# The least chosen score found by VectorE alone: a search in shares, with a threshold per partition, in six of eight batches

## The chip, the cores and the metric

The kernel runs on one core of a Trainium2 chip. The metric is the device time of one execution in microseconds. TensorE multiplies matrices into PSUM, VectorE, ScalarE and GpSimd work on tiles in SBUF, and SyncE issues nearly all transfers, in the order of its own queue.

## The reference

Eight batches of 3136 tokens. Each goes through an attention without softmax, and 128 of its tokens, those with the highest gate score, through a small network of two layers.

```python
scores = scale * np.matmul(z, z.transpose(0, 2, 1))     # z: 8 x 3136 x 64
attn = np.maximum(scores, 0.0) ** 2
x = u * np.matmul(attn, v)                              # u, v: 8 x 3136 x 256
gate = np.einsum('bsd,d->bs', x, w_gate)
for b in range(B):
    top_idx = np.argpartition(-gate[b], capacity)[:capacity]      # capacity 128
    xe = x[b, top_idx]
    ye = np.maximum(xe @ w1, 0.0) @ w2                  # 256 -> 1024 -> 256
    g = 1.0 / (1.0 + np.exp(-gate[b, top_idx]))
    out[b, top_idx] = x[b, top_idx] + g[:, None] * ye
```

## The kernel before

A batch is cut into seven chunks of output tokens: five of 512, one of 256 and one of 320. A chunk walks over all 3136 tokens in thirteen slots: twelve of two groups of 128 tokens and one of the last 64. In a slot TensorE multiplies the squared scores with `v` into `acc` (L523), with `hi` and `lo`, the two parts of each score, and in between computes the raw scores `sc` of the slot three ahead (L417). ScalarE takes these through a relu (L427) and rounds their square to `hi` (L428); VectorE squares them exactly (`a`, L438) or ScalarE does (L433), by what the planner thinks each has to do; VectorE or GpSimd subtracts to get `lo` (L487). Scores are symmetric, so VectorE also transposes squares that a later chunk needs (`aT`, L456, L475), they are stored (`squares`, `squares_narrow`, `squares_own`) and fetched there as old pairs, which need no score matmul. The score banks in PSUM are two, `acc` has three, and one bank, `misc`, is left for all small work.

The end of a chunk (`finish`) multiplies with `u`, transposes, stores and adds up the gate scores of its tokens; these are near tasks, in slots 2 and 5 of the next chunk. When a batch's last chunk is through, `route(b)` gives a list of far tasks, which run in the slots of the next batch: at most one per slot, none in a chunk's last slot, none in a slot with a near task, and after each a distance in slots that the list itself names (two where it names none). A task has matmuls, mixed into those of the slot, and posts, work for the other engines, put out around the work on the slot's scores (`settle_scores`): of several, the first half ahead of it and the rest behind; of one, it is ahead. Posts of the slot before a chunk's last one are held for that last one. The order on each engine is the order of issue. `spend` tells the planner what an engine was given, which decides between VectorE, ScalarE and GpSimd for squares and subtractions.

The search for the 128th highest score, in `route`: `fold` (L686) brings the scores of a batch into 98 rows of 32 and `start` copies them to `G`. Eight rounds then settle four bits each of the score's pattern. `tries` (L703) makes fifteen thresholds, `count` compares 98x15x32 elements (`ge`, L710) and adds up along each row (`cnt`, L718), `total` (L724) sums the rows with one matmul of a matrix of ones, and `settle` counts how many thresholds still have 128 scores or more (L729, L733) and appends that digit to `base` (L746 or L748). A round is one task with the distance three: `total`, then `settle` and `tries`, then `count`. After the last one come `masks` (which scores are above, which equal) and `run_up`, then `ahead`, `quotas`, `spans`, `take`, and the expert stage `expert` with its gather, two layers and scatter.

Batch 7 is different (`merged`): its last four chunks are searched late, and its first three through this search on 96 rows of 16. Batch 6 has its tasks at a distance of two, and the later part of batches 5 and 6's experts is held for the end.

Of the kernel before, what the change touches and what calls it, by code (L numbers as in the profile page):

```python
# [18 lines left out]
P = 128  # L19
# [21 lines left out]
def constants(S, cap):  # L41
# [35 lines left out]
    steps = np.arange(1, 1 << BITS, dtype=np.int64)  # L77
# [4 lines left out]
    return [np.concatenate(cols[dt], 1) for dt in (F32, BF16)], at, np.tile(keys, (rows, 1))  # L82


@with_exitstack
def attention_then_routed_ffn(ctx: ExitStack, tc: tile.TileContext, zt, ut, v, wg, w1, w2, cst, cst16, keys, outs, at, cap):
# [13 lines left out]
    NF = F // P  # L100
    SCALE = 1.0 / S
    NS = (1 << BITS) - 1
    SLOTS = NJ // 2 + 1

    const = ctx.enter_context(tc.tile_pool(name="const", bufs=1))
# [9 lines left out]
    def misc_bank(name):  # L115
        return ps_m.tile([P, 512], F32, name=name, tag="misc")
# [10 lines left out]
    def load_consts():  # L127
        c_sb = const.tile([P, cst.shape[1]], F32, name="c_sb")
        nc.sync.dma_start(c_sb, cst)
        k_sb = const.tile([TP, keys.shape[1]], I32, name="k_sb")  # L130
# [200 lines left out]
        for i in range(2)  # L331
    ]
    own = [[tc.dram_tile([P, GT, P], F32, name=f"squares_own{i}_{c}") for c in range(WHOLE)] for i in range(2)]

    def is_first(k):
        b, c, js, _ = slots[k]
# [329 lines left out]
    def route(b):  # L666
# [29 lines left out]

        def tries(rd):
            f = st["ps"][:R, 128 : 128 + NS]
            k = consts["keys"][:R, rd * NS : (rd + 1) * NS]
            if rd == 0:  # L700
                nc.vector.tensor_copy(f, k.bitcast(F32))
            else:
                nc.vector.tensor_scalar(f.bitcast(I32), k, st["base"], None, op0=ALU.bitwise_xor)  # L703
            st["f"] = f
            spend(dve=0.2)

# [15 lines left out]
        def total():  # L722
            st["ps"] = misc_bank("tot")
            nc.tensor.matmul(st["ps"][:R, :NS], ones, st["n"], start=True, stop=True)  # L724

        def settle(rd):
            junk = moe.tile([TP, NS], F32, name="enough", tag="enough")[:R]
            m = moe.tile([TP, 1], F32, name="m", tag="m")[:R]
            nc.vector.tensor_scalar(  # L729
                junk, st["ps"][:R, :NS], float(cap), None, op0=ALU.is_ge, op1=ALU.add, accum_out=m  # L730
            )
            mi = moe.tile([TP, 1], I32, name="mi", tag="mi")[:R]
            nc.vector.tensor_copy(mi, m)  # L733
            base = moe.tile([TP, 1], I32, name="base", tag="base", bufs=2)[:R]
            if rd == last:
                base = st["ps"][:R, 64:65].bitcast(I32)
            if rd == 0:
                k = moe.tile([TP, 1], I32, name="place", tag="place")[:R]
                nc.vector.tensor_scalar(
                    k, mi, 32 - BITS, INT_MIN, op0=ALU.logical_shift_left, op1=ALU.bitwise_xor  # L740
                )
                flip = moe.tile([TP, 1], I32, name="flip", tag="flip")[:R]
                nc.vector.tensor_scalar(
                    flip, k, 31, 0x7FFFFFFF, op0=ALU.arith_shift_right, op1=ALU.bitwise_and
                )
                nc.vector.tensor_tensor(base, k, flip, op=ALU.bitwise_xor)  # L746
# [5 lines left out]
            spend(dve=0.6)  # L752

        def masks():
            t = st["base"].bitcast(F32).broadcast_to([R, NT])
# [90 lines left out]
        for rd in range(last):  # L846
            tasks.append(([total], [lambda rd=rd: (settle(rd), tries(rd + 1)), count], 3))
        if late:
            tasks.append(([total], [lambda: settle(last), masks]))
            tasks += [([columns], keep_columns), ([places], ranks)]  # L850
            tasks += choose(st, 0, cap)
            choice[b] = st
        else:
            tasks.append(([total], [lambda: settle(last), masks, run_up]))
# [612 lines left out]
```

## Time and profile before

| | |
|---|---|
| time, median of 3 runs | 2091.34 us (2090.43 to 2091.94) |
| profiled execution, its own time | 2093.4 us |
| its span | 2091.6 us |
| TensorE busy | 2074.4 us, 99% |
| VectorE busy | 1511.1 us, 72% |
| GpSimd busy | 1370.5 us, 66% |
| ScalarE busy | 1278.5 us, 61% |
| mean DMA rate over the span | 196 GB/s |

Busy times are unions of an engine's instructions over one profiled execution. PE is TensorE, PEld its weight load, DVE VectorE, ACT ScalarE, POOL GpSimd, SP or SPq SyncE and its queue. L724 is line 724 of the kernel. "x4" is a count of instructions. In a timeline, a bracket gives the engine's idle time just before the instruction and what ended it. Matmuls are pipelined, so their durations overlap: distances are read from start to start.

### The profile page before, as it was taken

The page shows a single profiled execution, that of the slowest core. Times are in us where ns is not written, and L with a number is a line of the kernel's source. Part 1 is how long each engine was busy: PE and PEld are TensorE (multiplying, and loading weights), DVE is VectorE, ACT ScalarE, POOL GpSimd, SP SyncE. Part 2 cuts the span into 40 slices and gives each one's busy share as a digit, 9 for nine tenths or more (in the row PEclk, how much of TensorE's full clock was granted, in tenths as well). Part 3 has the DMA queues.
Part 4 walks back from the last instruction along what each step waited for, and adds up shares of the span by engine and source line. Part 5 has one row for each costly group of instructions (what it writes and reads, how often), then busy time and mean ns, then how long its engine had stood idle before and what let it go on. Part 6 is the DMA issues. An engine that isn't in the chain of part 4 may idle for free.

```text
span 2091.6 us, 31263 instructions
## 1 busy us (share of the span) xinstructions
PE 2074.4 (99%) x10359; PEld 1749.5 (84%) x10359; DVE 1511.1 (72%) x2334; ACT 1278.5 (61%) x1619; POOL 1370.5 (66%) x729
## 2 busy tenths in 40 slices
PE   9999999999999999999999999999999999999998
PEld 6888978889888898888988889888898888878788
DVE  8766678766777667875678757786577876787776
ACT  7665577656765467664676546765477655775543
POOL 6666677656866478764776647865578655765643
PEclk9999999999999999999999999999999999999999
DMA  6788767786668866688667876678776786666862
GB/s 190 201 242 212 206 184 214 217 229 173 188 188 222 216 184 189 185 221 217 183 192 190 228 206 188 186 199 224 199 200 180 192 194 184 186 181 168 216 168 94
DMA packets 408771, 409.66 MB, mean 196 GB/s; under 512 B 129120, under 2 KB 320416, under 8 KB 405536
## 3 DMA queue, kind: packets, MB, share of 16 engines
q1 hardware_dynamic: 407552, 405.30, 71.4%
q0 software_dynamic: 768, 2.10, 0.3%
q8 instruction: 81, 1.33, 0.3%
q14 instruction: 82, 0.67, 0.1%
q10 hardware_dynamic: 288, 0.26, 0.0%
HBM read 235.31 MB, written 172.23 MB: 195 GB/s over the span
## 4 chain that ended last, share of the span: by engine, by line
PE 81%; DMA 6%; POOL 4%; issue 3%; ACT 2%; DVE 2%; SPq 1%; POOLq 0%; ACTq 0%; DVEq 0%
PE acc L523 67%; PE sc L417 12%; DMA vst<-in_v 4%; POOL lo L487 2%; POOL V L121 1%; ACT a L427 1%; DVE a L438 1%; ACT hi L428 1%; PE h L1106 1%; PE y L1150 1%; SPq L274 1%; DMA vst<-in_w 1%; POOL ZL L121 1%; DMA squares_narrow<-aT 0%; DVE aT L456 0%
## 5 line engine op out<-in xcount | busy, mean ns | idle before, releaser
L523 PE MATMUL acc<-hi,V 128*128 128x512 f32 (+2 forms) x5376 | 1224.9, 366 | 3.2 <-DVE ut L568 1.0
L487 POOL TENSOR_TENSOR lo<-a,hi 128x1024 fp32r<-128x1024 f32 (+1 forms) x335 | 748.8, 2238 | 597.3 <-DVE a L438 443.1
L523 PEld LDWEIGHTS acc<-hi,V 128*128 128x128 f32 x5376 | 929.4, 188 | 166.3 <-DVE ut L568 5.9
L523 PE MATMUL acc<-lo,V 128*128 128x512 f32 (+2 forms) x2688 | 664.1, 363 | 0.0
L427 ACT ACTIVATE a<-sc 128x1024 f32<-128x1024 f32 (+4 forms) x408 | 363.0, 890 | 488.2 <-PE sc L417 364.8
L438 DVE TENSOR_TENSOR a<-sc,a 128x1024 f32<-128x1024 f32 (+3 forms) x334 | 338.4, 1013 | 289.8 <-ACT hi L428 261.3
L523 PEld LDWEIGHTS acc<-lo,V 128*128 128x128 f32 x2688 | 471.4, 188 | 76.7 <-POOL lo L487 1.5
L395 ACT CAST hi<-qk 128x1024 fp32r<-128x1024 f32 (+2 forms) x320 | 276.1, 863 | 234.8 <-PE acc L523 205.7
L456 DVE STREAM_TRANSPOSE aT<-a 128x512 f32<-128x512 f32 (+1 forms) x520 | 341.1, 691 | 101.0 <-ACT a L433 69.9
L428 ACT ACTIVATE hi<-a 128x1024 fp32r<-128x1024 f32 (+4 forms) x408 | 377.4, 925 | 18.7 <-PE acc L523 2.1
L487 DVE TENSOR_TENSOR lo<-qk,hi 128x1024 fp32r<-128x1024 f32 (+2 forms) x212 | 335.8, 1594 | 54.3 <-ACT hi L395 52.3
L417 PE MATMUL sc<-Z,ZH 128*128 128x512 f32 (+2 forms) x760 | 281.9, 375 | 4.8 <-DVE a L438 4.5
L417 PE MATMUL sc<-Z,ZL 128*128 128x512 f32 (+2 forms) x760 | 278.2, 370 | 0.7 <-DVE ZL L121 0.7
L487 POOL TENSOR_TENSOR lo<-qk,hi 128x1024 fp32r<-128x1024 f32 (+2 forms) x108 | 203.2, 1884 | 51.8 <-ACT hi L395 40.9
L417 PEld LDWEIGHTS sc<-Z,ZH 128*128 128x128 f32 x760 | 142.6, 188 | 39.2 <-DVE a L438 12.0
L417 PEld LDWEIGHTS sc<-Z,ZL 128*128 128x128 f32 x760 | 142.6, 188 | 25.2 <-DVE ZL L121 1.1
L121 POOL TENSOR_TENSOR V<-vst,V 128x512 fp32r<-128x512 f32 x89 | 139.7, 1579 | 13.9 <-ACT V L120 13.4
L589 POOL TENSOR_TENSOR ut<-x,w_run 128x1024 f32<-128x1024 f32 (+2 forms) x52 | 130.0, 2499 | 15.9 <-DVE x L580 14.9
L433 ACT ACTIVATE a<-a 128x1024 f32<-128x1024 f32 x74 | 78.6, 1062 | 2.4
L568 DVE SCALAR_TENSOR_TENSOR ut<-acc,ut 128x512 f32<-128x512 f32 (+2 forms) x112 | 64.0, 612 | 19.5 <-PE acc L523 19.2
L121 POOL TENSOR_TENSOR ZL<-zst,ZH 128x512 fp32r<-128x512 f32 (+2 forms) x56 | 73.5, 1317 | 2.4 <-ACT ZH L120 2.1
L120 ACT CAST V<-vst 128x512 fp32r<-128x512 f32 x95 | 57.8, 609 | 21.1 <-DMA vst<-in_v 20.8
(175 smaller groups left out, 1039.1 us busy)
## 6 DMA issues: line engine op xcount, KB each, us to landing
squares<-aT SPq DMA_DIRECT2D x160, 512.0 KB
qk<-squares SPq DMA_DIRECT2D x320, 256.0 KB
squares_narrow<-aT SPq DMA_DIRECT2D x320, 128.0 KB
qk<-squares_narrow SPq DMA_DIRECT2D x80, 512.0 KB
vst<-in_v SPq DMA_DIRECT2D x190, 128.0 KB
out<-x SPq DMA_DIRECT2D x162, 128.0 KB
ut<-in_ut SPq DMA_DIRECT2D x40, 512.0 KB
squares_own<-aT SPq DMA_DIRECT2D x39, 256.0 KB
```

The lines of the kernel that those rows point to most:

```text
L121: (lo_on or nc.vector.tensor_tensor)(lo, src, hi.bitcast(F32), op=ALU.subtract)
L395: nc.scalar.copy(by(hi), src)
L417: nc.tensor.matmul(ps[:, q], z[:, j * P : (j + 1) * P], mov, start=z is ZH, stop=z is ZL)
L427: nc.scalar.activation(a, ps[:, :n], AF.Relu)
L428: nc.scalar.activation(pieces[0][0](hi), pieces[0][1], AF.Square)
L433: nc.scalar.activation(a, a, AF.Square)
L438: square = lambda: nc.vector.tensor_tensor(a[rows], ps[rows, :n], a[rows], op=ALU.mult)
L456: nc.vector.transpose(to, a[rows, q].rearrange("p (m t a) -> p m t a", t=GT, a=Q))
L487: on.tensor_tensor(view(lo), src, view(hi).bitcast(F32), op=ALU.subtract)
L523: nc.tensor.matmul(ac[h], w, mov, start=first and h not in started, stop=stop)
L568: nc.vector.scalar_tensor_tensor(xT[:, h, :w], acc[b, c][h], SCALE * SCALE, xT[:, h, :w], op0=ALU.mult, op1=ALU.mult)
L589: nc.gpsimd.tensor_tensor(wx, runs, consts["wg_run"].rearrange("p (o r) -> p o r", o=1).broadcast_to([P, NB, RUN]), op=ALU.mult,)
```

## The change

For batches 0 to 5 the search takes another form. The scores are stored to DRAM (`set_out`) and loaded back so that each of eight shares of 392 scores lies on sixteen partitions (`bring_back`). Each of the sixteen has a threshold of its own (the last one is not counted). A round is two tasks. `count_shares` compares a share with a threshold on each of 128 partitions and accumulates the count, then brings the 128 counts into each of 32 partitions by four 32x32 transposes. `settle_shares` adds up the eight shares, compares with 128, counts, appends the digit to the base, and makes the next threshold of each partition with four xors of 32 partitions. Its sums lie in the `misc` bank, written by VectorE. No matmul is in a round. The distance is one slot behind a count and one or two behind a settle.

Batches 6 and 7 keep the old form, but `tries` shifts one row of steps instead of reading shifted ones.

```diff
-    keys = np.concatenate(keys).astype(np.uint32).view(np.int32)
+    own = np.stack(keys, 1)
+    own[-1] = 0
+    own = np.tile(own, (P >> BITS, 1))
+    keys = np.concatenate([own, np.tile(np.append(keys[0], steps), (P, 1))], 1).astype(np.uint32).view(np.int32)
...
+        def set_out():
+            nc.vector.tensor_copy(G, st["ps"][:R, :NT])
+            stores.append(lambda: nc.sync.dma_start(scores_there[b % 2].rearrange("(r t) -> r t", t=NT), G))
+
+        def bring_back():
+            n = S // SHARES
+            st["row"] = moe.tile([P, 4, P], F32, name="gates", tag="hh", bufs=2).rearrange("p f r -> p (f r)")[:, :n]
+            for g in range(SHARES):
+                src = scores_there[b % 2][g * n : (g + 1) * n].rearrange("(o t) -> o t", o=1)
+                nc.sync.dma_start(st["row"][g << BITS : (g + 1) << BITS], src.broadcast_to([1 << BITS, n]))
+            st["least"] = consts["keys"][:, 0:1].bitcast(F32)
+
+        def count_shares():
+            big = moe.tile([P, 512], F32, name="ge", tag="big", bufs=2)
+            own = moe.tile([P, 1], F32, name="own", tag="m")
+            nc.vector.tensor_scalar(
+                big.bitcast(BF16)[:, : S // SHARES], st["row"], st["least"], None,
+                op0=ALU.is_ge, op1=ALU.add, accum_out=own,
+            )
+            st["n"] = big[:Q, 512 - P :]
+            for q in range(0, P, Q):
+                nc.vector.transpose(st["n"][:, q : q + Q], own[q : q + Q].broadcast_to([Q, Q]))
+            spend(dve=1.5)
+
+        def settle_shares(rd):
+            ps = misc_bank("tot")
+            n, enough = ps[:Q, : NS + 1], ps[:Q, 32 : 32 + NS]
+            nc.vector.tensor_reduce(n, st["n"].rearrange("p (g s) -> p s g", s=NS + 1), axis=AX.X, op=ALU.add)
+            nc.vector.tensor_scalar(enough, n[:, :NS], float(cap), None, op0=ALU.is_ge)
+            mi = moe.tile([Q, 1], I32, name="mi", tag="mi")
+            with nc.allow_low_precision(reason="whole numbers"):
+                nc.vector.tensor_reduce(mi, enough, axis=AX.X, op=ALU.add)
+            shift = 32 - BITS * (rd + 1)
...
+            base = moe.tile([Q, 1], I32, name="base", tag="base", bufs=2)
+            if rd == 0:
+                first_base(base, mi, Q)
+            else:
+                nc.vector.tensor_scalar(base, mi, shift, st["base"], op0=ALU.logical_shift_left, op1=ALU.bitwise_xor)
+            least = moe.tile([P, 1], I32, name="least", tag="least", bufs=2)
+            for q in range(0, P, Q):
+                nc.vector.tensor_scalar(
+                    least[q : q + Q], consts["keys"][:Q, rd + 1 : rd + 2], base, None, op0=ALU.bitwise_xor
+                )
+            st["base"] = base
+            st["least"] = least.bitcast(F32)
+            spend(dve=1.65)
...
-        last = 32 // BITS - 1
-        tasks = [([fold], [start, count], 3)]
+        last = ROUNDS - 1
+        by_shares = not late and not (put_off(b) and b == B - 2)
+        if by_shares:
+            tasks = [([fold], set_out, 2), ([], bring_back, 2)]
+            for rd in range(last):
+                tasks += [([], count_shares, 1), ([], lambda rd=rd: settle_shares(rd), 1 + rd % 2)]
+            tasks += [([], count_shares, 1), ([], [lambda: settle_shares(last), lambda: (masks(), run_up())], 2)]
+        else:
+            tasks = [([fold], [start, count], 3)]
+            for rd in range(last):
+                tasks.append(([total], [lambda rd=rd: (settle(rd), tries(rd + 1)), count], 3))
```

`first_base` holds the three instructions that `settle` had for round 0. The last settle writes its base to four groups of 32 partitions in PSUM, for `masks`, which stays as it was.

## Rows read from the trace of the kernel before

**Rows 1.** The profile's page: busy us of each engine with its share of the span and count of instructions, and the shares of the chain that ended last by engine.

```profile
PE 2074.4 (99%) x10359; PEld 1749.5 (84%) x10359; DVE 1511.1 (72%) x2334; ACT 1278.5 (61%) x1619; POOL 1370.5 (66%) x729
...
PE 81%; DMA 6%; POOL 4%; issue 3%; ACT 2%; DVE 2%; SPq 1%; POOLq 0%; ACTq 0%; DVEq 0%
```

**Rows 2.** The waits of TensorE over the whole span: who waited for whom, us in total, times, longest.

```profile
PE sc L417 <- DVE a L438: 4.5, 9, 0.8
...
PE tot L724 <- DVE cnt L718: 1.1, 2, 0.8
```

**Rows 3.** The timeline of TensorE in batch 1's search: start, us, line, operation.

```profile
574.00 1.07 PE L523 MATMUL acc<-lo,V 128*128 128x512 f32 x4
574.91 0.17 PE L724 MATMUL tot<-cnt,c 98*98 98x15 bf16 x1
...
576.86 0.39 PE L417 MATMUL sc<-Z,ZH 128*128 128x512 f32 x1
...
577.78 1.07 PE L523 MATMUL acc<-lo,V 128*128 128x512 f32 x4
...
580.50 0.39 PE L417 MATMUL sc<-Z,ZH 128*128 128x512 f32 x1
```

**Rows 4.** The instructions of the tile `tot` on TensorE (duration in ns: least, median, most; first and last start in us), and from the timeline the last one of batch 5's search (the 48th of the 64) and the first two of batch 6's.

```profile
L724 PE MATMUL tot<-cnt,c x64: 169/173/175, 309.7 to 1990.3; 98*98 98x15 bf16 x56, 96*96 96x15 bf16 x8
...
1664.48 0.17 PE L724 MATMUL tot<-cnt,c 98*98 98x15 bf16 x1
...
1831.71 0.17 PE L724 MATMUL tot<-cnt,c 98*98 98x15 bf16 x1 [0.77 <-DVE cnt L718]
...
1839.27 0.17 PE L724 MATMUL tot<-cnt,c 98*98 98x15 bf16 x1 [0.37 <-DVE cnt L718]
```

**Rows 5.** Groups of VectorE by line and shape: the search's instructions. Busy us, mean ns of one, then the idle time before them.

```profile
L718 DVE TENSOR_REDUCE cnt<-ge 98x15 bf16<-98x480 bf16 x56 | 36.7, 656 | 1.9
...
L710 DVE TENSOR_TENSOR ge<-G,tot 98x480 bf16<-98x480 f32 x49 | 30.2, 617 | 0.0
...
L703 DVE TENSOR_SCALAR tot<-k_sb,base 98x15 int32<-98x15 int32 x49 | 11.6, 237 | 1.7
...
L748 DVE TENSOR_SCALAR base<-mi,base 98x1 int32<-98x1 int32 x42 | 9.0, 214 | 1.5
L733 DVE CAST mi<-m 98x1 int32<-98x1 f32 x56 | 8.6, 154 | 1.9
L729 DVE TENSOR_SCALAR_CACHE_REDUCE enough<-tot 98x15 f32<-98x15 f32 x56 | 8.6, 153 | 4.6 <-PE tot L724 4.3
...
L729 DVE DVE_READ_ACCUMULATOR enough<-tot 98x1 f32 x56 | 4.5, 81 | 0.0
```

**Rows 6.** The nearest shapes to the new instructions: from the same view a compare with accumulation of 384 columns and a reduction of 240, and from the views of the tiles `aT`, `mi` and `base` (duration in ns: least, median, most; first and last start) the transposes, the shift with xor of one column (L748) and the xor of two tiles (L746).

```profile
L954 DVE TENSOR_SCALAR_CACHE_REDUCE beats<-row,col 128x384 bf16<-128x384 f32 x4 | 2.4, 598 | 0.0
...
L718 DVE TENSOR_REDUCE cnt<-ge 96x15 bf16<-96x240 bf16 x8 | 3.2, 401 | 0.3
...
L456 DVE STREAM_TRANSPOSE aT<-a x520: 662/702/717, 19.1 to 2013.5; 128x512 f32<-128x512 f32 x162, 64x512 f32<-64x512 f32 x12
...
L475 DVE STREAM_TRANSPOSE aT<-a x78: 399/418/447, 58.2 to 1980.4; 128x256 f32<-128x256 f32 x78
...
L748 DVE TENSOR_SCALAR base<-mi,base x48: 210/214/216, 318.8 to 1978.8; 98x1 int32<-98x1 int32 x42, 96x1 int32<-96x1 int32 x6
...
L746 DVE TENSOR_TENSOR base<-place,flip x8: 156/681/1727, 313.8 to 1953.4; 98x1 int32<-98x1 int32 x7, 96x1 int32<-96x1 int32 x1
```

**Rows 7.** Busy time by stretch: the stretch and its length, then busy us (and count) of PE, PEld, DVE, ACT and POOL, the granted clock, the DMA share and GB/s. First a stretch of batch 0's search, a part of batch 1's, and all of batch 6's; then the sum over the seven searches of batches 0 to 6, 83 us each and 65 for the last.

```profile
314.00:391.00 77.00, 77.00 (x347) 63.01 (x347) 63.06 (x120) 51.37 (x58) 56.86 (x28) 1.00 0.71 199
585.00:605.00 20.00, 20.00 (x92) 16.40 (x92) 18.52 (x31) 11.94 (x15) 13.75 (x7) 1.00 0.79 210
1823.00:1888.00 65.00, 63.86 (x285) 51.18 (x284) 53.97 (x110) 45.30 (x52) 42.26 (x24) 1.00 0.62 176
...
sum 563.00, PE 561.86 PEld 458.20 DVE 461.24 ACT 377.16 POOL 386.50; mean PE 80.27 PEld 65.46 DVE 65.89 ACT 53.88 POOL 55.21
```

**Rows 8.** The timeline of a score bank in the second chunk of batch 1's search: the scores, the relu, the square, and the score matmul two groups on, which takes the same bank.

```profile
597.63 0.39 PE L417 MATMUL sc<-Z,ZH 128*128 128x512 f32 x1
...
598.80 1.03 ACT L427 ACTIVATE a<-sc 128x1024 f32<-128x1024 f32 x1 [2.03 <-PE sc L417]
...
601.01 1.23 DVE L438 TENSOR_TENSOR a<-sc,a 128x1024 f32<-128x1024 f32 x1 [0.16 <-ACT hi L428]
...
604.50 0.39 PE L417 MATMUL sc<-Z,ZH 128*128 128x512 f32 x1
```

**Rows 9.** The timeline of SyncE's queue, and below it of VectorE, around the end of the first chunk after batch 0.

```profile
304.41 4.08 SPq L470 DMA_DIRECT2D squares_narrow<-aT  x6
310.85 0.34 SPq L477 DMA_DIRECT2D squares_own<-aT  x1
316.00 0.52 SPq L462 DMA_DIRECT2D squares<-aT  x1
...
310.05 0.77 DVE L475 STREAM_TRANSPOSE aT<-a 128x256 f32<-128x256 f32 x2 [0.96 <-DMA squares_narrow<-aT]
...
317.12 1.29 DVE L456 STREAM_TRANSPOSE aT<-a 128x512 f32<-128x512 f32 x2
```

**Rows 10.** The timeline of SyncE's queue: four loads of 64 KB issued one after the other.

```profile
329.82 2.02 SPq L385 DMA_DIRECT2D vst<-squares_own  x4
```

More of the change, by code (lines that the diff above doesn't have):

```diff
@@ L76, in constants @@
     put("tok_late16", tok.reshape(P, -1), BF16)
-    steps = np.arange(1, 1 << BITS, dtype=np.int64)
+    steps = np.arange(1, (1 << BITS) + 1, dtype=np.int64)
     keys = [(steps << sh) & 0xFFFFFFFF for sh in range(32 - BITS, -1, -BITS)]
@@ L80, in constants @@
     keys[0] = np.where(keys[0] >> 31, keys[0] ^ 0x7FFFFFFF, keys[0])
-    keys = np.concatenate(keys).astype(np.uint32).view(np.int32)
-    return [np.concatenate(cols[dt], 1) for dt in (F32, BF16)], at, np.tile(keys, (rows, 1))
+    own = np.stack(keys, 1)
+    own[-1] = 0
+    own = np.tile(own, (P >> BITS, 1))
+    keys = np.concatenate([own, np.tile(np.append(keys[0], steps), (P, 1))], 1).astype(np.uint32).view(np.int32)
+    return [np.concatenate(cols[dt], 1) for dt in (F32, BF16)], at, keys
 @with_exitstack
@@ L102, in attention_then_routed_ffn @@
     NS = (1 << BITS) - 1
+    ROUNDS = 32 // BITS
+    SHARES = P >> BITS
     SLOTS = NJ // 2 + 1
@@ L129, in load_consts @@
         nc.sync.dma_start(c_sb, cst)
-        k_sb = const.tile([TP, keys.shape[1]], I32, name="k_sb")
+        k_sb = const.tile([P, keys.shape[1]], I32, name="k_sb")
         nc.sync.dma_start(k_sb, keys)
@@ L333, in attention_then_routed_ffn @@
     own = [[tc.dram_tile([P, GT, P], F32, name=f"squares_own{i}_{c}") for c in range(WHOLE)] for i in range(2)]
+    scores_there = [tc.dram_tile([S], F32, name=f"scores{i}_there") for i in range(2)]
     def is_first(k):
@@ L724, in total, with first_base @@
             nc.tensor.matmul(st["ps"][:R, :NS], ones, st["n"], start=True, stop=True)
+        def first_base(base, mi, n):
+            k = moe.tile([TP, 1], I32, name="place", tag="place")[:n]
+            nc.vector.tensor_scalar(k, mi, 32 - BITS, INT_MIN, op0=ALU.logical_shift_left, op1=ALU.bitwise_xor)
+            flip = moe.tile([TP, 1], I32, name="flip", tag="flip")[:n]
+            nc.vector.tensor_scalar(flip, k, 31, 0x7FFFFFFF, op0=ALU.arith_shift_right, op1=ALU.bitwise_and)
+            nc.vector.tensor_tensor(base, k, flip, op=ALU.bitwise_xor)
         def settle(rd):
@@ L737, in settle @@
             if rd == 0:
[L738 to L746, printed above, removed]
+                first_base(base, mi, R)
             else:
@@ new lines, in settle_shares @@
+        def settle_shares(rd):
[7 more added lines that the diff above has]
+            shift = 32 - BITS * (rd + 1)
+            if rd == last:
+                least = ps[:, 64:65].bitcast(I32)
+                for q in range(0, P, Q):
+                    nc.vector.tensor_scalar(
+                        least[q : q + Q], mi, shift, st["base"], op0=ALU.logical_shift_left, op1=ALU.bitwise_xor
+                    )
+                st["base"] = least[:R]
+                spend(dve=1.45)
+                return
+            base = moe.tile([Q, 1], I32, name="base", tag="base", bufs=2)
[4 more added lines that the diff above has]
+            least = moe.tile([P, 1], I32, name="least", tag="least", bufs=2)
+            for q in range(0, P, Q):
+                nc.vector.tensor_scalar(
+                    least[q : q + Q], consts["keys"][:Q, rd + 1 : rd + 2], base, None, op0=ALU.bitwise_xor
+                )
+            st["base"] = base
+            st["least"] = least.bitcast(F32)
+            spend(dve=1.65)
@@ L840, in take @@
             nc.tensor.matmul(st["ps"][:, : NT + 2], st["of"], st["taken"], start=True, stop=True)
-        last = 32 // BITS - 1
-        tasks = [([fold], [start, count], 3)]
+        last = ROUNDS - 1
[9 more added lines that the diff above has]
+                tasks.append(([total], [lambda rd=rd: (settle(rd), tries(rd + 1)), count], 3))
         if late:
             tasks.insert(0, ([], [lambda: bring_weight(1), halve]))
-        for rd in range(last):
-            tasks.append(([total], [lambda rd=rd: (settle(rd), tries(rd + 1)), count], 3))
-        if late:
             tasks.append(([total], [lambda: settle(last), masks]))
@@ L853, in route @@
         else:
-            tasks.append(([total], [lambda: settle(last), masks, run_up]))
+            if not by_shares:
+                tasks.append(([total], [lambda: settle(last), masks, run_up]))
             tasks.append(([ahead], [quotas, lambda: spans(0)], 3))
```

7 lines of the change are left out of this document (4 added, 3 removed).

## The prediction

> **What bounds the kernel now.** I read the busy times first. TensorE is busy for 2074.4 of a span of 2091.6 us, VectorE for 1511.1 (72%) [rows 1]; the chain of work that ended last is TensorE for 81% of its length [rows 1]. The reader is to see that nothing but TensorE's own stream can give a microsecond back, unless another engine makes it wait. Next I read TensorE's waits. The largest is the score matmuls waiting for VectorE's square, 4.5 us in 9 waits; the search's own matmul (`tot`) waited 1.1 us in two [rows 2], and both of those lie in the search that keeps the old form [rows 4]. So in the six batches of the change no wait on the search is to be won: the search costs TensorE only what its matmuls occupy. Third I read one such matmul in its surroundings, and last VectorE's load in the stretch where the search runs.
>
> **What is removed from TensorE.** Each round has one 98x15 matmul, 64 in the kernel; the six changed batches hold 48 of them, the first at 309.7 us and the last at 1664.48 [rows 4]. The busy row says 0.17 us for one, but it overlaps its neighbours, so I take start to start. With it, from the four `lo` matmuls at 574.00 to the next score matmul at 576.86, it is 2.86 us; the same sequence without it, one slot on, runs from 577.78 to 580.50, 2.72 us [rows 3]. The price is 0.14 us, most of it behind the matmul: its 15 columns are too short to cover the next weight load. 48 x 0.14 = **6.7 us**, and it lies wholly on the path, since TensorE is busy for 77.00 of 77 us there at a granted clock of 1.00, its 2.4 GHz level [rows 7].
>
> The Trainium skill speaks against this gain: by its page "TensorE: Matmul & The Clock Gate", section "Back-to-back issue gap", a matmul of 1 to 64 columns has an issue floor of about 25 ns. By that the 48 would be worth an estimated 1.2 us; the row shows 140 ns, and the sum goes by the row.
>
> **What is added to VectorE.** Before, a round is 0.153 (`enough`) + 0.081 (its accumulator read) + 0.154 (`mi`) + 0.214 (`base`) + 0.237 (the tries) + 0.617 (`ge`) + 0.656 (`cnt`) = 2.11 us [rows 5]. After, none of the new shapes is in the trace. *Count*: a compare with accumulation over 392 columns; 384 columns took 0.598 [rows 6], so 0.61, with an accumulator read of 0.08. Then four transposes of 32 columns: 512 columns take 0.702 and 256 take 0.418 [rows 6], a slope of 1.1 ns a column and some 0.14 fixed, so 0.17 each and 0.12 start to start where one does not need the other; 0.5 in all, **1.2 us**. *Settle*: a reduction of 128 elements, from 0.656 at 480 and 0.401 at 240 some 0.28; compare and reduction of 15, 0.15 each as `enough` and `mi`; the base 0.21 as L748; four xors of which only the first waits for the base, 0.21 + 3 x 0.12 [rows 5, 6]; with 0.04 between dependent ones, **1.6 us**. A round is thus 2.8 to 2.9 us against 2.11. Bounds: 2.3 (every small one overlapped down to 0.1) to 4.2 (each of the dozen small ones the 0.21 of L748, none overlapped); I take 2.9, because neighbouring independent instructions overlap in the trace.
>
> Where it lands: by the slot rules the fold stays in slot 8 of the next batch's first chunk; the eight counts then take slots 0, 3, 6, 8 and 11 of the second chunk and 1, 6 and 8 of the third, the settles 1, 4, 7, 9 and then 0, 3, 7 and 9. That is the stretch 314 to 391 us for batch 0. VectorE is busy for 63.06 of its 77 us [rows 7], 13.9 idle. The old search has about seven and a half rounds there, 15.8 us; the new one 8 x 2.9 = 23.2. The 7.4 more fit, and leave VectorE at 91%. The window 585 to 605 has it at 93% (18.52 of 20) with TensorE busy for all 20.00 [rows 7], so such a load alone does not hold TensorE up. The planner sees the load too (1.5 + 1.65 us declared against 2.2 before) and will send some squares to ScalarE and subtractions to GpSimd, which the same window has at 11.94 and 13.75 of 20 [rows 7].
>
> The finer test is the lag. A score bank must be squared before the score matmul two groups on. The tightest place inside the stretch: scores at 597.63, square at 601.01 to 602.24, bank wanted at 604.50 [rows 8]: 2.26 us to spare. Up to there, from slot 4 of that chunk, the new form has done settle, count, settle, count, 5.6 us; the old one two rounds, 4.2. The square can come 1.4 us later at most: still 0.8 to spare. The third chunk has more work moved into it, and its old pairs, which need no score bank, lie between. So I put the new waits at nothing, with 0.5 us for what I overlook. The cover that is lost is that 0.8: a round dearer by over half of it is paid by TensorE.
>
> The search ends some three slots later (`ahead` in slot 11 of the third chunk, not 8), and so does the expert stage; its matmuls are the same ones and have a whole batch's slots, so this costs nothing.
>
> **The queue of SyncE.** Nine transfers come in per batch: the scores out (12.5 KB), behind the fold, and eight broadcast loads of 25 KB two slots later. SyncE issues four small loads in 2.02 us [rows 10], so eight are about 4 us. It reaches them after the narrow stores that run from 304.41 to 308.49; only the store of the chunk's own squares at 310.85 is queued behind them, and then nothing until 316.00 [rows 9]. That store slips by under 2 us. The loads wait for the scores' landing, but these were issued some 5 us earlier; a store's landing held VectorE's transpose until 310.05 [rows 9], at most 1.6 us after the last narrow store's issue ended and 5.6 after the first's began. The first count stands in slot 0 of the second chunk, near 314.4 us; if the loads land at 316 to 318, VectorE waits 2 to 4 us with the transposes of 317.12 behind it [rows 9]; squares in those slots are ScalarE's, so TensorE is not behind that wait. Cost: 0 to 1 us a batch, taken as 0.
>
> **Sum.** -6.7 + 0.5 = -6.2 us. The profiled execution stands at 2093.4 us with its span of 2091.6 in it, 2.1 above the median of 2091.34; I set the difference against the median: **2085.1 us**.
>
> **Rivals.** *Given back in small waits*: rounds cost 3.6 us rather than 2.9, so the lag passes the 2.26 in one or two places per batch. Batch 6's search, at two slots a round, lost 65.00 - 63.86 = 1.14 us of TensorE [rows 7], mostly on `tot` itself, at 0.77 and 0.37 [rows 4], but for VectorE's lag. At 0.5 to 1.1 in each of six batches 3 to 6.6 us come back: 2087.5 to 2091. For it: 91% load; against it: over the seven old stretches together TensorE lost 563.00 - 561.86 = 1.14 us, all of it in batch 6's [rows 7]. Chance 0.14.
>
> *The small matmul is nearly free*: if the 0.14 were a feature of the stream that stays when the matmul goes, as 25 ns each would have it, 2090. The pair of sequences speaks against it. Chance 0.03. The page's floor, named above, is this case.
>
> *VectorE is held by GpSimd, slower*: the first round's `base`, a xor of two tiles, takes 156 ns at best, 681 in the median and 1727 at most [rows 6], which looks like a hold by another engine. If the compare from and to SBUF, or the four xors, were held the same way, each by 0.5 us (681 - 156), a round costs 2 x 0.5 more, 8 us a batch on top of the 7.4: 15.4 against 13.9 idle, and locally past the 0.8 us. From two holds a round on it decides; TensorE would then lose 2 to 3 us a batch, 12 to 18 in all: 2097 to 2103. Against it: L748, the same kind of instruction, took 210 to 216 ns in all 48 cases [rows 6]. Chance 0.05. The Trainium skill's page "SBUF — State Buffer", section "SBUF: two separate sides", has the rule: VectorE in a two-port mode, or with two SBUF inputs, and GpSimd lock each other out of one pair of ports for a whole instruction; by it the xor's long cases are explained, and the one-input compare would be at risk only in a two-port mode, which 0.598 us for 384 columns does not look like.
>
> *The loads come late*: 5 us or more of VectorE's wait at the first count, and with it the own-squares store; TensorE loses 1 to 2 us a batch, 2091 to 2097. Chance 0.04.
>
> **How the numbers follow.** The forecast itself has 0.74: its own range is 2083 (a matmul at 0.17, 48 x 0.17 = 8.2, no wait) to 2087. With the first rival the range for 8 in 10 reaches to **2083 to 2091**. 0.2% is 4.2 us, about what a measurement of this kernel tells from no change, so faster means below 2087.2: 0.74 and a little of the first rival, **0.76**; same, the most of the first, the second, half the last: **0.16**; slower **0.08**.
>
> **What the profile after would show.** 16 `tot` matmuls left of 64; slots in the stretch 2.72 us where they were 2.86; VectorE's busy time up by 30 to 45 us, ScalarE's or GpSimd's by a few; no `sc` wait for a square inside the six stretches. Waits of TensorE on the square at 320 to 390 us, a compare of more than 0.7 us, or a first count that waits for `gates` would each name the rival that holds.

## The result, and the profile after

The changed kernel takes 2105.3 us (median of six runs, 2104.36 to 2109.43) against 2092.28 beside it (2090.43 to 2094.71): the ratio is 1.0066, interval 1.0053 to 1.0079. It is slower by 13 us, where 2085.1 was forecast with a range that ended at 2091. The profiled execution is the slowest of the six: 2109.43 us, with a span of 2107.7.

The page of the changed kernel: busy times, and the shares by engine of the chain that ended last.

```profile
PE 2074.4 (98%) x10311; PEld 1750.3 (83%) x10311; DVE 1567.9 (74%) x2646; ACT 1282.9 (61%) x1624; POOL 1381.2 (66%) x742
...
PE 64%; DMA 10%; issue 7%; POOL 6%; DVE 6%; ACT 5%; SPq 2%; POOLq 0%; DVEq 0%; ACTq 0%
```

Beside [rows 1]: 48 matmuls fewer, yet TensorE is busy for the same 2074.4 us, and the span is 16.1 longer. Its idle time went from 17.2 us (2091.6 - 2074.4) to 33.3. It is in the chain for 64% of the way where it was for 81%: others now end later than it, here and there. The waits of TensorE in the changed kernel tell who:

```profile
PE sc L423 <- DVE a L444: 6.1, 9, 1.2
PE acc L529 <- POOL lo L493: 6.1, 6, 1.1
PE taken L908 <- DVE of L902: 6.0, 6, 1.0
PE h L1181 <- ACT hr L1191: 3.6, 5, 0.7
PE acc L529 <- DVE ut L574: 1.7, 1, 1.7
```

The square, which the prediction watched, is up from 4.5 to 6.1 [rows 2]. The next three rows are of another kind, waits of nearly equal length that return from batch to batch: six at `take`, five at the first layer, and five of the six on `lo`, behind the scatter (the sixth, 0.83 us, lies in batch 0's search). `take` and the first layer belong to the stages behind the search, which the change does not edit.

To place the loss I matched the 1520 score matmuls of the two traces in order and took, where a group of them begins, the start after minus the start before (us). This is worked out from the timelines; batch 2's part:

```
before   after    offset  step
 812.21   821.89    9.68          ahead of the search
 835.19   844.80    9.61  -0.13   seven such steps (-0.12 to -0.14), one
 ...                              of -0.17 and one of +0.13
 901.37   910.18    8.81  -0.17   the search is through
 918.38   928.52   10.14  +1.32   behind `take`
 975.76   986.91   11.15  +0.50   both layers are through (+1.01 since take)
1002.87  1015.29   12.42  +1.31   behind the scatter
```

The first part is the forecast: each matmul that is gone gives 0.13 us, 0.9 in the batch net (the one step of +0.13 was not followed up). The rest takes back 3.6. Steps of the same size stand in all batches that have the stage: +1.33 six times (8.0), about +1.05 between five times (5.2), +1.31 five times (6.6), 19.8 us in all. At each of the three places the step is some 0.3 us longer than the wait that the trace shows (1.00, 0.72 and 1.04): the waits there sum to 14.9 us of the 19.8, and the rest lies in time that counts as busy, and goes some way to explain why TensorE is busy for as long as before. What makes it up was not traced.

A further +3.07 falls at 184 to 188 us, ahead of any search. Two things are in it: a wait of 1.72 us (0.99 before), and behind it a granted clock of 0.50, the 1.2 GHz level, from 186.8 to 190.2. The profiled execution of the second experiment below, with the old kernel's code up to there, has the wait (1.70) with the clock at 1.00, and a step of only 0.8. I put the +3.07 down to the execution and not to the change; the other five runs of this kernel lie 2 to 5 us lower.

*Take.* The timeline of the changed kernel at the first of the three places, in batch 1 (TensorE, VectorE and GpSimd, lines of each in order of time):

```profile
657.41 0.17 PE L868 MATMUL ahead<-upto,c 98*98 98x2 bf16 x1
...
659.36 2.41 POOL L493 TENSOR_TENSOR lo<-a,hi 128x1024 fp32r<-128x1024 f32 x1 [4.95 <-DVE a L444]
...
660.39 0.15 DVE L877 TENSOR_SCALAR quota<-ahead 98x1 f32<-98x1 f32 x1
...
660.77 1.02 DVE L879 TENSOR_TENSOR quota<-quota 98x1 f32<-98x1 f32 x1
...
661.73 2.40 POOL L493 TENSOR_TENSOR lo<-qk,hi 128x1024 fp32r<-128x1024 f32 x1
...
661.82 2.36 DVE L882 SCALAR_TENSOR_TENSOR taken<-upto,quota 98x32 bf16<-98x32 bf16 x1
...
665.62 0.35 DVE L902 SCALAR_TENSOR_TENSOR of<-c_sb,quota,ahead 98x128 bf16<-98x128 f32 x1
...
666.03 0.19 PE L908 MATMUL taken<-taken,of 98*128 98x34 bf16 x1 [1.00 <-DVE of L902]
```

The matmul `ahead` runs at 657.41, in slot 11 of the third chunk. The posts of that slot are held for the chunk's last one, so `quotas` begins only at 660.39, 2.8 us after its matmul's end. There L879 and L882 stretch to 1.02 and 2.36 us, each to the end of the subtraction that GpSimd has under way (661.77 and 664.13); by themselves they take 0.16 and 0.25 (last section). `of` starts at 665.62, and TensorE stands for 1.00 us.

*First layer.* The timeline of the changed kernel in batch 2's expert stage (ScalarE, TensorE):

```profile
962.36 0.59 ACT L1191 ACTIVATE hr<-h 128x512 f32<-128x512 f32 x1
...
963.00 0.50 PE L1181 MATMUL h<-wh,xh 128*128 128x512 f32 x1 [0.72 <-ACT hr L1191]
```

The layer's first half now lies in slot 11 of the fourth chunk. Its rectification `hr` is held, `misc` is a single bank, and the matmul of the second half waits 0.72 us for the bank.

*Scatter.* The timeline of the changed kernel one chunk on (VectorE, GpSimd, TensorE):

```profile
1004.88 0.48 DVE L1231 SCALAR_TENSOR_TENSOR y<-y,g,xe 128x256 f32<-128x256 f32 x1
...
1005.64 1.01 POOL L1235 DMA_INDIRECT out<-y,ids  x1 [11.61 <-DVE y L1231]
1006.67 2.51 POOL L493 TENSOR_TENSOR lo<-qk,hi 128x512 fp32r<-128x512 f32 x2
...
1008.00 0.74 PE L529 MATMUL acc<-lo,V 128*128 128x256 f32 x4 [1.04 <-POOL lo L493]
```

`y` is a post of slot 11 of the fifth chunk and held as well. The scatter is next in GpSimd's queue and stands for it for 11.61 us, with the subtractions of `lo` behind it. They are due in the sixth chunk, whose narrow slots (256 columns) take half the time and give half the cover.

Last, the new shapes on VectorE, for which the prediction had only bounds, from the views of the tiles `ge` and `least` of the changed kernel (duration in ns: least, median, most; first and last start):

```profile
L787 DVE STREAM_TRANSPOSE ge<-own x192: 199/200/205, 317.1 to 1690.7; 32x32 f32<-32x32 f32 x192
L793 DVE TENSOR_REDUCE tot<-ge x48: 329/340/360, 320.4 to 1693.8; 32x16 f32<-32x128 f32 x48
L781 DVE TENSOR_SCALAR_CACHE_REDUCE ge<-gates,least x42: 577/605/622, 329.0 to 1689.4; 128x392 bf16<-128x392 f32 x42
...
L815 DVE TENSOR_SCALAR least<-k_sb,base x168: 200/204/209, 321.7 to 1689.2; 32x1 int32<-32x1 int32 x168
```

And the window of batch 0's search in the changed kernel, columns as in [rows 7]:

```profile
314.00:393.00 79.00, 78.17 (x345) 63.77 (x344) 65.80 (x168) 51.96 (x59) 62.00 (x31) 1.00 0.70 198
```

TensorE lacks 0.83 us of 79, one wait on `lo` at 358.53 in this batch. But for that the search stays fed.

### The profile page after: what moved, and what is told of

It reads as the page before. It is cut to its first block, busy times and chain, and to the rows that moved or that the text cites. A ratio compares the mean times of both kernels' runs of the same rounds, so it can differ in the third digit from the quotient of the medians.

```text
span 2107.7 us, 31537 instructions
## 1 busy us (share of the span) xinstructions
PE 2074.4 (98%) x10311; PEld 1750.3 (83%) x10311; DVE 1567.9 (74%) x2646; ACT 1282.9 (61%) x1624; POOL 1381.2 (66%) x742
## 3 DMA queue, kind: packets, MB, share of 16 engines
q8 instruction: 81, 1.33, 0.3%
## 4 chain that ended last, share of the span: by engine, by line
PE 64%; DMA 10%; issue 7%; POOL 6%; DVE 6%; ACT 5%; SPq 2%; POOLq 0%; DVEq 0%; ACTq 0%
PE acc L529 52%; PE sc L423 11%; POOL lo L493 4%; DMA vst<-in_v 4%; ACT a L433 2%; ACT hi L434 2%; DVE a L444 2%; DMA squares_narrow<-aT 2%; DMA qk<-squares 2%; DVE aT L462 1%; POOL ZL L126 1%; POOL V L126 1%; DMA squares<-aT 1%; SPq L391 1%; DVE taken L882 1%
## 5 line engine op out<-in xcount | busy, mean ns | idle before, releaser
L493 POOL TENSOR_TENSOR lo<-a,hi 128x1024 fp32r<-128x1024 f32 (+1 forms) x335 | 740.3, 2213 | 563.3 <-DVE a L444 439.6
L444 DVE TENSOR_TENSOR a<-sc,a 128x1024 f32<-128x1024 f32 (+5 forms) x329 | 332.6, 1011 | 270.1 <-ACT hi L434 231.7
L493 POOL TENSOR_TENSOR lo<-qk,hi 128x1024 fp32r<-128x1024 f32 (+2 forms) x115 | 220.4, 1921 | 35.9 <-ACT hi L401 19.9
L439 ACT ACTIVATE a<-a 128x1024 f32<-128x1024 f32 x79 | 83.9, 1062 | 2.5
L126 POOL TENSOR_TENSOR ZL<-zst,ZH 128x512 fp32r<-128x512 f32 (+2 forms) x56 | 64.7, 1160 | 10.1 <-ACT ZH L125 8.5
```

The source lines that it names most:

```text
L126: (lo_on or nc.vector.tensor_tensor)(lo, src, hi.bitcast(F32), op=ALU.subtract)
L439: nc.scalar.activation(a, a, AF.Square)
L444: square = lambda: nc.vector.tensor_tensor(a[rows], ps[rows, :n], a[rows], op=ALU.mult)
L493: on.tensor_tensor(view(lo), src, view(hi).bitcast(F32), op=ALU.subtract)
```

## The experiments

The theory after the result: the loss is that of the **later stages**, which the search's three more slots push into slots whose posts are held. The rivals: the new round's load on VectorE costs the time (directly, or through what the planner hands to the others); the small matmul's price was never 0.14.

**The old slots.** The new rounds are one task each, spaced so that the last one has its old slot (6 of the third chunk) and all that follows keeps its place.

```diff
-            for rd in range(last):
-                tasks += [([], count_shares, 1), ([], lambda rd=rd: settle_shares(rd), 1 + rd % 2)]
-            tasks += [([], count_shares, 1), ([], [lambda: settle_shares(last), lambda: (masks(), run_up())], 2)]
+            for rd, gap in enumerate((3, 3, 2, 2, 3, 3, 3)):
+                tasks.append(([], [count_shares, lambda rd=rd: settle_shares(rd)], gap))
+            tasks.append(([], [count_shares, lambda: (settle_shares(last), masks(), run_up())], 2))
```

> The changed kernel with count and settle of a round in one slot (count ahead of the slot's own squares, settle behind them) and distances between rounds that bring the stage that follows the search (ahead, take, the expert) back to the very slots that it had before the change. VectorE's instructions are those of the changed kernel. Theory A (the loss is where the later stages now stand): the 48 matmuls' 6.7 us are kept and the waits of TensorE on `of`, on `hr` and on `lo` behind the scatter are gone: 2084 to 2087 us, ratio 0.996 to 0.998. Theory B (the loss is VectorE's heavier search, 92% of its time in that stretch, which makes everything behind it late): the same work in the same stretch, so 2100 us or more.

Measured: 2102.26 us, ratio 1.0045 (1.0031 to 1.0059). By its time this is the load rival's result (2100 or more), and the theory's 2084 to 2087 missed. The waits of TensorE have to say why:

```profile
PE ahead L868 <- DVE upto L861: 9.8, 6, 1.6
PE acc L529 <- POOL lo L493: 9.0, 6, 1.7
```

Waits on `of`, on `hr` and behind the scatter are gone, as the theory wants. Two others took their place. One is at the turn to the third chunk, where a settle and a count stand ahead of a square and TensorE waits for the `lo` made from it. The other is at `ahead`, one slot behind a last step that is now a count, a settle, the masks and two scans. VectorE ends the scans at 907.36 (905.31 + 2.05), and the matmul has waited for them, as this kernel's timeline (GpSimd, VectorE, TensorE) shows:

```profile
904.76 1.29 POOL L493 TENSOR_TENSOR lo<-vst,hi 128x512 fp32r<-128x512 f32 x1
...
905.31 2.05 DVE L861 TENSOR_TENSOR_SCAN upto<-mk 98x32 bf16<-98x32 bf16 x2
...
906.01 1.27 POOL L126 TENSOR_TENSOR ZL<-zst,ZH 128x512 fp32r<-128x512 f32 x1
...
907.41 0.16 PE L868 MATMUL ahead<-upto,c 98*98 98x2 bf16 x1 [1.64 <-DVE upto L861]
```

The two scans are old instructions with two inputs, and they are stretched like L879 and L882: 2.05 us for both, ending with GpSimd's second subtraction (907.28), where the changed kernel has 0.34 (at 656.01). The 1.71 us more is as much as the wait. So the edit's packing put them beside GpSimd's work; that the wait would go without the stretching was not tried.

**Only the delay.** The old kernel with its old search, and the step behind it three slots later.

```diff
-            tasks.append(([total], [lambda: settle(last), masks, run_up]))
+            tasks.append(([total], [lambda: settle(last), masks, run_up], 5))
```

> The kernel before, search and matmuls untouched, with a distance of five slots in place of two behind the last round of the six batches, so that the stage that follows starts in slot 11 of the third chunk, as in the changed kernel. Theory A: it shows the price of the place alone, 1.33 us a batch at `take` and 2.3 us at the expert in five of them: 6 x 1.3 + 5 x 2.3 = 19, so about 2110 us, ratio 1.008 to 1.010. Theory B: a delay costs nothing, 2090 to 2093 us.

Measured: 2110.19 us, ratio 1.0084 (1.0068 to 1.0099), as the theory had it. The waits of TensorE hold the same three rows, with no new instruction in the program:

```profile
PE taken L840 <- DVE of L834: 5.4, 6, 0.9
PE acc L523 <- POOL lo L487: 5.2, 5, 1.1
PE h L1106 <- ACT hr L1116: 3.6, 5, 0.7
```

So 18.3 us (2110.19 - 2091.94) come from moving a stage whose work is unchanged. Less the 6 of the matmuls that makes 12, close to the 13 of the result. The page's busy times answer the load rival as well:

```profile
PE 2077.3 (98%) x10359; PEld 1748.9 (83%) x10359; DVE 1552.2 (74%) x2339; ACT 1278.2 (61%) x1619; POOL 1360.2 (64%) x724
```

VectorE is busy for 41.1 us more than before [rows 1] without a new round: most of the 56.8 that it has more in the changed kernel comes with the stage's place, not with the search.

**No hold.** The changed kernel, and posts are no longer held for a chunk's last slot (batch 7 excepted).

```diff
             posts, held_posts = [now], [fn for fn in posts if fn is not settle_scores]
+            if not late:
+                posts, held_posts = [now, *held_posts], []
```

> The changed kernel, but the posts of slot 11 are not held for slot 12: they are put out in slot 11, behind its squares, in batches 0 to 6. The stages stay in slot 11. Theory A in its narrow form (the hold is what makes slot 11 dear): the waits on `of`, `hr` and the late `lo` go, 2086 to 2091 us. Theory A in its wide form (slot 11 itself, with the end of the chunk behind it, is dear): 2098 to 2105. Theory B: no change, 2105.

Measured: 2111.41 us, ratio 1.009 (1.0074 to 1.0105), above all that was expected. The three waits are gone, but the chunk's end pays. First the wait in this kernel's view of TensorE's waits:

```profile
PE acc L529 <- DVE ut L574: 18.1, 7, 2.8
```

Then its longest case in TensorE's timeline:

```profile
923.08 2.07 PE L529 MATMUL acc<-hi,V 128*128 128x512 f32 x4 [2.79 <-DVE ut L574]
```

The multiplication with `u` frees an `acc` bank; with the far tasks' posts ahead of it in VectorE's order it is late. L879 is among them and stretched here too, to 2.18 us (918.93 to 921.11, beside a subtraction of GpSimd's from 918.72 to 921.10). And behind four of the six such waits the granted clock falls to 0.50, the 1.2 GHz level, for 3.4 us, as two windows from the start of the slow stretch and of its like (columns as in [rows 7]) show:

```profile
922.70:926.10 3.40, 3.02 (x7) 2.44 (x8) 2.71 (x5) 0.86 (x1) 0.00 (x0) 0.50 0.27 92
1446.10:1449.50 3.40, 3.40 (x15) 2.83 (x16) 2.33 (x4) 1.80 (x2) 0.00 (x0) 1.00 0.39 107
```

Matched with the kernel before, the step at these four is +4.65 to +4.87 us, and +3.2 at the two where the clock stays at 1.00: some 1.6 us each, 6.2 in all, about what this kernel lies above the changed one (6.1). So the three waits hang on the hold, but taking it away brings another wait of like size and the slow clock, and is not the remedy.

**The stage two slots later still.** The changed kernel with one number changed, so that `ahead` falls into slot 0 of the fourth chunk.

```diff
-            tasks += [([], count_shares, 1), ([], [lambda: settle_shares(last), lambda: (masks(), run_up())], 2)]
+            tasks += [([], count_shares, 1), ([], [lambda: settle_shares(last), lambda: (masks(), run_up())], 4)]
```

> The changed kernel with a distance of four slots in place of two behind its last settle, so that `ahead` starts in slot 0 of the fourth chunk instead of slot 11 of the third, and what follows moves too (gather, the layers and the scatter some four to five slots later). The search is untouched. Theory A with slot 11 as its core: the wait on `of` goes, 1.3 us in six batches, and the one on `hr`, 0.7 to 1.0 in five; the scatter now falls among the narrow slots of the sixth chunk, where it may hold GpSimd as before or more: 2088 to 2098 us. Theory B: nothing changes in the search, so about 2105.

Measured: 2086.07 us (2084.99 to 2090.71), ratio 0.9976 (0.9967 to 0.9985): 19.2 below the change, lower than the 2088 to 2098 expected, and faster than the kernel before by 5.9. The search's code is the changed kernel's, and so is VectorE's load in its stretch (63.99 us from 314 to 391, against 64.01). The page of this kernel, busy times and the chain by engine:

```profile
PE 2071.4 (99%) x10311; PEld 1750.3 (84%) x10311; DVE 1521.9 (73%) x2641; ACT 1285.3 (62%) x1624; POOL 1394.2 (67%) x747
...
PE 82%; DMA 5%; POOL 3%; ACT 3%; issue 3%; DVE 3%; SPq 1%; POOLq 0%; ACTq 0%; DVEq 0%
```

And its longest waits of TensorE:

```profile
PE sc L423 <- DVE a L444: 3.6, 6, 1.3
PE acc L529 <- DVE ut L574: 1.7, 1, 1.7
```

Of the three rows only the wait on `lo` in batch 0's search is left (0.82 us), and TensorE is back at 82% of the chain. VectorE's total is 46.0 us below the changed kernel's: L879 and L882 account for 17.8 of that, as they are not stretched here, and the rest was not followed up. The stage's place thus changes VectorE's load too, outside the search.

**The rounds earlier.** The first experiment's single tasks, but spaced so that the rounds end early and the last step has four slots.

```diff
-            for rd, gap in enumerate((3, 3, 2, 2, 3, 3, 3)):
+            for rd, gap in enumerate((1, 2, 1, 3, 2, 5, 3)):
...
-            tasks.append(([], [count_shares, lambda: (settle_shares(last), masks(), run_up())], 2))
+            tasks.append(([], [count_shares, lambda: (settle_shares(last), masks(), run_up())], 4))
```

> The first kernel again (a round in one slot, later stages in their old slots), but with the eight rounds at slots 0, 1, 3, 4, 7 and 9 of the second chunk and 1 and 4 of the third, where it had 0, 3, 6, 8, 10 and 0, 3 and 6. No round stands at the turn of the chunks, and the last one has four slots ahead of `ahead` instead of two. The first kernel lost 1.64 us a batch to `ahead` waiting for `upto` and 1.4 to 1.7 to a `lo` of GpSimd at the turn. Theory A (each loss is one wait at one place, which goes when its work is moved): both are gone and the matmuls' 6.5 us are left: 2084 to 2088 us, ratio 0.996 to 0.9985. Theory B (VectorE is simply given too much, and what it loses comes out somewhere): 2098 us or more, in other waits on VectorE or GpSimd.

Measured: 2088.02 us, ratio 0.998 (0.9971 to 0.9989). The wait at `ahead` is gone; the one on `lo` is left at 5.9 us in six waits, 1.7 the longest, at the turn of a chunk. No round has a slot at the turn now, yet in batch 2 a settle (868.29 to 870.20) still stands straight ahead of the square whose `lo` the matmul at 873.98 waits for, by 0.83 us where it was 1.38. So a round can be packed into one slot, and what is ahead of that square counts; that no more than this makes the wait was not shown.

**Each count twice**, once on the first experiment and once on the kernel with the stage later still: the load rival by itself. Every count is made a second time with the same result, some 1.5 us more of VectorE in each of 48 rounds and 1.5 more declared to the planner. In both the eight tasks of a batch get this edit (shown for the second kernel's first seven):

```diff
-                tasks += [([], count_shares, 1), ([], lambda rd=rd: settle_shares(rd), 1 + rd % 2)]
+                tasks += [([], lambda: (count_shares(), count_shares()), 1), ([], lambda rd=rd: settle_shares(rd), 1 + rd % 2)]
```

> The first of these kernels (count and settle in one slot, later stages in their old slots) with each count made twice, the second one over the first: 48 counts of about 1.5 us more for VectorE, 12 us in each search, more than its idle time there. Theory A with room to spare in the lag: under 2 us over the first of these kernels. Theory B: VectorE's load is what counts, so at least 10 us over the first.

Measured: 2130.57 us, ratio 1.0182 (1.0166 to 1.0197), 28.3 above the first experiment. TensorE now waits 17.5 us in all for the scans at `ahead`, and 10.7 for `ut`. The wait at `ahead` is 2.9 us long, and behind it, in five of the six batches, the granted clock stands at 0.50 for 3.4 or 6.8 us. Matched with the first experiment, the step there is 1.3 us in the batch without it and 2.7 to 4.1 in the others: some 10 of the 28 us are the clock.

> The kernel with the stage behind the search moved to slot 0 of the fourth chunk, and each count in the six batches made twice: some 12 us more for VectorE in each search. If only the places of waits count and the search has room, under 3 us over that kernel, 2086 to 2089 us. If VectorE's load is near a limit there, TensorE waits in the search stretches themselves, 10 us or more over it.

Measured: 2094.98 us, ratio 1.0015 (1.0006 to 1.0024), 8.9 above the same kernel without it, between what the two theories said. The same load costs 28 us (some 18 but for the clock) in one arrangement and 9 in the other. Where the load lands in the second, by its window (columns as in [rows 7]):

```profile
314.00:391.00 77.00, 76.69 (x339) 62.75 (x337) 66.08 (x201) 54.97 (x61) 62.05 (x30) 1.00 0.70 201
```

VectorE is at 66.08 us, only 2.1 above the 63.99 that the kernel with one count has there: ScalarE took 3.8 more (51.13 there) and GpSimd 2.0 (60.00). Of the 12 us that eight counts add, 8 show as busy time here; the rest was not traced. TensorE's new waits are two a batch, about 0.5 us each, at the turn out of that stretch (391 and 397 us). Load is thus not free, but it is not what the change lost its time to.

**The matmul twice.** The old kernel, with the sum's matmul of the six batches made a second time, into columns that nobody reads.

```diff
+        def again():
+            nc.tensor.matmul(st["ps"][:R, 256 : 256 + NS], ones, st["n"], start=True, stop=True)
...
+        more = [] if late or b == B - 2 else [again]
...
-            tasks.append(([total], [lambda rd=rd: (settle(rd), tries(rd + 1)), count], 3))
+            tasks.append(([total, *more], [lambda rd=rd: (settle(rd), tries(rd + 1)), count], 3))
...
-            tasks.append(([total], [lambda: settle(last), masks, run_up]))
+            tasks.append(([total, *more], [lambda: settle(last), masks, run_up]))
```

> The kernel before with the sum of each round in the six batches made twice: the same 98x15 matmul a second time, at another place in the same slot and into unread columns of the same bank; nothing else is moved. It prices the removed matmul by itself. By the prediction's 0.14 us: 48 x 0.14 = 6.7 us more, 2098 to 2100 us, ratio 1.003. By an issue floor of 25 ns each: 1.2 us more, no difference that can be measured.

Measured: 2102.39 us, ratio 1.0052 (1.0038 to 1.0065), 10.7 us slower and over the 2098 to 2100 expected. Matched as above, 42 of the 48 places show a step of +0.09 to +0.16, nearly all +0.12, 5.1 us together. The other six, one in each search, hold a wait of the edit's own (+0.83 to +1.37, 6.7 together): with two matmuls in the slot the earlier one moves up to mid-slot, where in a search's second round its counts are not yet there (TensorE's timeline of this kernel):

```profile
835.85 0.21 PE L724 MATMUL tot<-cnt,c 98*98 98x15 bf16 x1 [0.54 <-DVE cnt L718]
838.08 0.17 PE L727 MATMUL tot<-cnt,c 98*98 98x15 bf16 x1
```

This happens six times, 4.9 us in all by the view of the waits. The price of the matmul held (0.12 for 0.14); the place of one in each search cost about as much as all the extra ones.

## Why the prediction was wrong, step by step

**What TensorE saves** was right: 0.14 us a matmul foretold, 0.13 in the offsets of the search, 0.12 where it is doubled; 48 x 0.13 = 6.2 us against 6.7. The rival of a nearly free matmul falls. The Trainium skill's page "TensorE: Matmul & The Clock Gate", section "Back-to-back issue gap", gives an issue floor of about 25 ns for so few columns, and says beside it that in a stream of matmuls with weight loads the spacing is set by both. The 0.13 us measured for one such matmul between wide ones is above that floor and does not contradict it; the floor is no price.

**What VectorE is given** was sized too low, inside its bounds. From the timeline of the first experiment a count is 1.50 us (871.48 to 872.98) and a settle 1.87 (867.50 to 869.37): 3.37 a round against 2.9. The four transposes take 0.84 and the four xors 0.86, 0.21 from start to start: independent, yet not overlapped. The prediction had this for its upper bound, and took 0.12. The compare (605 ns, 0.61 foretold) was right. VectorE's busy time rose by 56.8 us and not by 30 to 45, but 41.1 came with the delay alone.

**The lag** held in the search of five batches and broke once, 0.83 us in batch 0. The rival *given back in small waits* named rounds of 3.6 and waits on the square inside the stretches; the rounds came near, the waits did not. Nor did the prediction's own bound hold, that a round dearer by over half of 0.8 us is paid by TensorE: 3.37 is dearer by 0.47, and five searches paid nothing.

**SyncE's queue** was right at 0: no `gates` wait; the loads land in 1.7 us, the first count is at 316.5.

**The step that failed** is this one: "The search ends some three slots later (`ahead` in slot 11 of the third chunk, not 8), and so does the expert stage; its matmuls are the same ones and have a whole batch's slots, so this costs nothing." The slot was worked out correctly, and the rule that posts of the slot before a chunk's last one are held stood in the description of the kernel; the two were not put together. The stage has slots enough, but a task there is a matmul with work behind it that the next task needs, and in slot 11 this work starts a slot late (at `take`, GpSimd's hold on VectorE comes on top). The distances of the stage, fitted to slot 8, carried two more steps into a slot 11 (the first layer, `y`). Cost: 19.8 us by the offsets, 18.3 with the delay alone, 19.2 when it is taken away. The sum with it, -6.2 + 0.8 + 19.8 = +14.4, stands near the +13.0 measured; the remainder is not split further.

**The rival on the slower side** had a mechanism that is there, at another place. It asked whether GpSimd holds the new instructions: it does not, 168 xors took 200 to 209 ns and 42 compares 577 to 622. Held are two old instructions with two tiles as inputs, far more since the stage moved: before, L879 (L811 there) took 159 ns in the mean and L882 (L814) 1069, now 894 and 2061 (last section). It foretold 2097 to 2103 from two holds in each round; the time came near that from elsewhere, and it is not credited.

**Left open.** How much of the 1.00 us at `take` is the hold of posts and how much GpSimd's stretching was not separated. The stretching by itself does not make the wait: without the hold L879 still takes 2.18 us and TensorE does not wait at `take`. Whether the hold by itself would, no run shows; the stretching lengthens the way to `of` by 3.0 us there, three times the wait. The square's waits in a batch's first chunk (4.5 us over the whole span before, 6.1 after) were not followed up.

## What to carry to other kernels

When steps of a schedule are added or taken away, write down the slot of every later step, to the end of the stage, and read the rules of those slots (held posts, a single bank, an in-order queue) before calling a shift free; "it has time enough" says nothing about places. A stage's own delay can be tried alone in one line, on the old kernel as well as on the new one, and so parts a change's work from its side effect on the schedule. Matching the same instructions of two traces and reading where the offset steps shows gains and losses that cancel in the sum, which the list of waits does not.

## What the runs showed of the hardware

Two instructions of VectorE on tiles of one or 32 columns took as long as GpSimd's subtraction beside them. In the changed kernel L879 (98x1) took 1.02 us and ended at 661.79, L882 (98x32) 2.36 and ended at 664.18; GpSimd's two subtractions end at 661.77 and 664.13. In the kernel with the stage two slots later, whose GpSimd is idle from 660.83 to 662.02, the same two (VectorE's timeline) are short:

```profile
661.07 0.16 DVE L879 TENSOR_TENSOR quota<-quota 98x1 f32<-98x1 f32 x1
...
661.27 0.25 DVE L882 SCALAR_TENSOR_TENSOR taken<-upto,quota 98x32 bf16<-98x32 bf16 x1
```

The Trainium skill's page "SBUF — State Buffer", section "SBUF: two separate sides", says that VectorE with two inputs from SBUF and GpSimd lock each other out for a whole instruction; the trace agrees here, 1.02 against 0.16 us and 2.36 against 0.25, and the compare with one tile as input was free of it.

The two scans of the first experiment are a third case, 2.05 us against 0.34.

VectorE's four transposes of 32x32 elements and its four xors of 32x1 start 0.21 us apart though none needs the last: 0.84 us for the one, 0.86 for the other. It is not so for all small instructions: L879 above and L880 behind it (661.15, 98x1) start 0.08 us apart.

TensorE's granted clock fell from the 2.4 GHz to the 1.2 GHz level behind some long waits: for 3.4 us behind four of six waits of 2.8 us in the kernel without the hold, where it cost some 1.6 us each, and behind one of 1.72 us in the changed kernel. Behind the waits of 1.4 to 1.75 us in the first experiment it stayed at 1.00. What separates the two cases, no run shows.
